# An attention-and-gated-MLP kernel: y returned in transposed form, gating and spatial sums read PSUM on VectorE, late u, a plain first spatial product

## The chip, the cores and the metric

The kernel runs on one core of one Trainium2 chip. The metric is device time in microseconds. In the profile PE is TensorE (PEld its weight loads), DVE is VectorE, ACT is ScalarE, POOL is GpSimd, SP is SyncE, which issues the DMAs.

## The reference

B = 4 batches, H = 8 heads, S = 768 tokens, D = 48. A linear attention with decay, and behind it a gated MLP that mixes tokens:

```python
for t in range(S):                                   # r, k, v: (B, H, S, D)
    cur = einsum('bhd,bhe->bhde', u * k[t], v[t])
    y[:, :, t] = einsum('bhd,bhde->bhe', r[t], state + cur)
    state = w[:, :, None] * state + einsum('bhd,bhe->bhde', k[t], v[t])
x = y as (B, S, 384)
h = maximum(x @ w_in, 0)                             # 384 -> 1024
u, v = h[..., :512], h[..., 512:]
v_n = (v - mean(v)) / sqrt(var(v) + 1e-6)            # over the 512 features
v_s = einsum('ts,bsd->btd', w_spatial, v_n) + b_spatial
out = (u * v_s) @ w_out                              # 512 -> 384
```

All is fp32. The large products are done as three products of high and low parts (high x high, high x low, low x high); such a triple is called `mm3`. A value that goes into such a product is first split: a cast gives the high part, and a subtraction the low part.

## The kernel before

**Scheduling.** The program does not emit instructions directly. `op()` records an operation with the engines that may do it and a planned duration on each. `plan.run()` then simulates the engines: TensorE takes the ready operation that was written first, the other engines take by due time, and an operation that VectorE or GpSimd may do goes to one of them by these rules. `plan.issue()` emits the result, so each engine has a fixed order. Buffers come from numbered groups (`gF` ten 128x384 buffers for u, sums and outputs; `gAB` ten double ones for split operands; `gX` four for x; `gM` four PSUM banks, shown as `pm`; `ps` and `xp` two banks each). An operation that needs a slot waits for the last reader of what was in it.

**Attention.** A batch has six chunks of 128 tokens, 24 in all, and `attend(m)` does one: `prep` scales k and r by the decays (L513, 128x512 each), makes the products r k u (L515, L516; for the first seven chunks `prod` on L522 and column sums on TensorE, L532) and ks (L517), and from their sums dg (L538) the diagonal blocks of the matrix a (`dia`, L541). `g0` (L548 from `s`) multiplies r of the first 64 tokens with the carried state. `g1` makes the scores (L578) and the state's gains (L586) in `ps`. `mid` merges the scores into a with a predicated copy (L595) and forms t1, ub and s2, the state after 64 and after 128 tokens (L603, L607, L609). `g2` (L548) adds t1's share for the second 64 tokens and a x v, both into `xp`, as y with tokens on the partitions. Then yh (a cast, ACT or DVE) and yl = y - yh follow (L636 on VectorE; in the first seven chunks L631 on TensorE and a copy), and `turn` (L650) transposes both through TensorE with an identity, from where they are copied (L309 on ACT or L313 on DVE) into xh and xl, the halves of x. A half batch (three chunks) has one xh and one xl.

**MLP.** `moe_v` (one per chunk, nine 128x512 matmuls, L660 to L662) gives v; relu, statistics and scales follow (L684 to L717), and the normalization runs on ACT (L724) or DVE (L726). `moe_u` (half batch t, feature block d) gives u by nine 128x384 matmuls, copied to SBUF with relu. The spatial product over 768 tokens runs in seven products instead of eight, `moe_sp(b, k, n)`, with k a pair of feature blocks and n the unit:

```python
UNITS = {1: ("X", "11", "11"), 7: ("Y", "s3", "t3"), 5: ("Z", "s1", "t1"), 2: ("X", "12", "21"),
         6: ("Y", "s2", "t2"), 4: ("Y", "22", "t4"), 3: ("Z", "s4", "22")}
```

The three entries are the PSUM bank, the data operand and the weight operand. A unit is nine 128x384 matmuls (L809). Its data operands are blocks of v or sums of them (`s3`, L739; `tail`, L754), each split by `apart` (high on ACT, low part L734 on DVE or POOL). Its weight operands are blocks of the spatial weights or differences of them (`conv_sp`, L479), split likewise (L475 the low part). The sums behind a unit are on L821: with a PSUM operand they run on VectorE, with both operands in SBUF on VectorE or GpSimd:

```python
op({"V": vec(TH)} if xp else VP, lambda e: e.tensor_tensor(out=o(), in0=x(), in1=y(), op=alu),
```

`gate` then multiplies the sum by u in SBUF (L790), and splits the result, gt (ACT, and L793 for the low part). `moe_out` multiplies gt by w_out (twelve 128x384 matmuls), and the result is copied (`ob`) and stored.

**Order.** Batch 0's chunks 0 to 6 are written by hand among the conversions of the weights and the first v and u units. From there a list `seq` holds the units of all batches (v, outputs of the batch before, u, spatial units), and an attention step is put in after every 34/6 of its units.

Of the kernel before, what the change touches and what calls it, by code (L numbers as in the profile page):

```python
# [75 lines left out]

class Plan:
# [81 lines left out]
    def run(self, t0, late=0.4):  # L159
# [3 lines left out]
        idle = {e: 0.0 for e in "EAVPS"}  # L163
        wire = 0.0
# [5 lines left out]
        while pend:  # L170
            while True:
                began = False
                for e in "EAVPS":
# [3 lines left out]
                    for o in ready:  # L177
# [7 lines left out]
                        k = o.i if e == "E" else o.due  # L185
# [8 lines left out]
                    idle[e] = t + o.eng[e]  # L194
                    o.end = idle[e] + o.lag
# [58 lines left out]
def fused_kernel(ctx, tc, rkT, rkvN, wT, uB, w_in, w_sp, b_sp, w_out, out):  # L254
# [34 lines left out]
    def vec2(n):  # L289
        return (n + 150) / 960 + 0.09  # L290
# [32 lines left out]
    eye, neg, one = fixed([P, P], "eye"), fixed([P, P], "neg", F32R), fixed([P, P], "one", F32R)  # L323
    diag, mask, w128 = fixed([P, HC], "diag"), fixed([P, 2, HC], "mask"), fixed([P, NP], "w128")
# [3 lines left out]
    ws = {n: fixed([P, 2, 3, TH], f"ws{n}", F32R) for n in ("11", "21", "22", "t1", "t2", "t3", "t4")}  # L328

# [7 lines left out]
    def load_chunk(m, parts):  # L337
# [29 lines left out]
    def raw_out(k):  # L367
        raws["out", k] = buf = Buf(gAB, [P, 2 * TH], U32, "raw", "c", 3)
# [32 lines left out]
    op({"A": sb(128)}, lambda e: e.mul(neg(), eye(), -1.0), r=[eye], w=[neg], name="neg")
    op({"A": sb(128)}, lambda e: e.copy(one(), eye()), r=[eye], w=[one], name="one")

    def turn_tt(p, z, s0):
        pt = Buf(gM, [P, 512], F32, "pm", "t", 1)

        def f(e):
            for j in range(2):
                hd, o = slice(64 * j, 64 * j + 64), s0 ^ 64 * j
                e.matmul(pt()[o:o + 64, 0:64], tt()[hd, p, s0:s0 + 64], eye()[hd, hd], start=True, stop=True,  # L410
                         skip_group_check=True)

        op({"E": 0.2}, f, r=[tt, eye], psum=[pt], name="tn")
        acopy((tn, (p, z)), lambda: tn()[:, p, z, :], pt, lambda: pt()[:, 0:D], D, True, "tn", {"V": vec(D)})
# [65 lines left out]

    def conv_sp(i):
# [24 lines left out]
    def prep(m):  # L506
# [10 lines left out]
        op(VP, lambda e: e.tensor_tensor(out=kn()[:, 0:DM], in0=kn()[:, 0:DM], in1=tn().rearrange("s p z d -> s (p z d)"),  # L517
# [507 lines left out]
```

## Time and profile before

| | |
|---|---|
| three runs | 403.17, 397.26, 399.00 us; median 399.0 us |
| profiled execution | 399.85 us, its span 398.0 us |
| TensorE clock granted, mean | 0.965 |
| busy share PE, DVE, ACT, POOL | 91%, 77%, 38%, 60% |
| instructions in the span | 11111 |
| DMA | 38.66 MB, mean 97 GB/s |

The page gives the busy time of each engine over the span, the clock in 40 slices, the groups of instructions that cost most and, for each, the idle time ahead of it with what ended it. A share is a mean over the span: weights are loaded and converted, and batch 0 runs, in about its first third, and the outputs of batch 0 begin at 138 us.

### The profile page before, as it was taken

The page shows a single profiled execution, that of the slowest core. Times are in us where ns is not written, and L with a number is a line of the kernel's source. Part 1 is how long each engine was busy: PE and PEld are TensorE (multiplying, and loading weights), DVE is VectorE, ACT ScalarE, POOL GpSimd, SP SyncE. Part 2 cuts the span into 40 slices and gives each one's busy share as a digit, 9 for nine tenths or more (in the row PEclk, how much of TensorE's full clock was granted, in tenths as well). Part 3 has the DMA queues.
Part 4 walks back from the last instruction along what each step waited for, and adds up shares of the span by engine and source line. Part 5 has one row for each costly group of instructions (what it writes and reads, how often), then busy time and mean ns, then how long its engine had stood idle before and what let it go on. Part 6 is the DMA issues. An engine that isn't in the chain of part 4 may idle for free.

```text
span 398.0 us, 11111 instructions
## 1 busy us (share of the span) xinstructions
PE 361.5 (91%) x4686; PEld 330.6 (83%) x4686; DVE 304.6 (77%) x522; ACT 149.8 (38%) x355; POOL 240.5 (60%) x210
## 2 busy tenths in 40 slices
PE   2989999977977699998997999999979999999996
PEld 1868797876976699987987899888879899989996
DVE  4958899998999962769999744789999913579840
ACT  3436464734343221434341312336241322443421
POOL 4877887994998850756997423338998400116520
PEclk9989998986999999999998999999998999999999
DMA  7998255502120243252222334324031011000012
GB/s 227 336 294 273 74 155 173 182 23 91 26 91 0 83 132 99 76 161 70 94 68 68 95 112 135 102 68 145 20 114 49 2 61 41 21 0 2 1 34 86
DMA packets 24385, 38.66 MB, mean 97 GB/s; under 512 B 2960, under 2 KB 16528, under 8 KB 24336
## 3 DMA queue, kind: packets, MB, share of 16 engines
q1 hardware_dynamic: 24336, 37.96, 30.2%
q8 instruction: 37, 0.61, 0.7%
q14 instruction: 12, 0.10, 0.1%
HBM read 33.23 MB, written 4.72 MB: 95 GB/s over the span
## 4 chain that ended last, share of the span: by engine, by line
PE 52%; DVE 32%; issue 6%; POOL 4%; DMA 3%; ACT 1%; SPq 1%; DVEq 0%; POOLq 0%
PE pm L660 11%; PE pm L661 10%; PE pm L662 10%; PE pm L809 6%; PE xp L548 6%; DVE tp L821 5%; DVE ab L734 4%; DVE sf L754 3%; PE pm L650 2%; PE ps L578 2%; PE ps L586 2%; DVE v L726 1%; DMA uw<-wT 1%; DVE u L790 1%; PE pm L456 1%
## 5 line engine op out<-in xcount | busy, mean ns | idle before, releaser
L809 PE MATMUL pm<-wst,ab 128*128 128x384 f32 x288 | 59.2, 351 | 4.5 <-DVE ab L734 2.0
L809 PEld LDWEIGHTS pm<-wst,ab 128*128 128x128 f32 x288 | 52.0, 196 | 6.8 <-DVE ab L734 3.0
L809 PE MATMUL pm<-ws,ab 128*128 128x384 f32 x216 | 43.8, 352 | 0.0
L734 POOL TENSOR_TENSOR ab<-v,ab 128x384 fp32r<-128x384 f32 x19 | 23.4, 1233 | 32.2 <-ACT ab L309 32.2
L809 PEld LDWEIGHTS pm<-ws,ab 128*128 128x128 f32 x216 | 39.3, 196 | 0.2
L660 PE MATMUL pm<-xh,wiuh 128*128 128x384 f32 x96 | 34.9, 363 | 0.0
L660 PE MATMUL pm<-woh,gt 128*128 128x384 f32 x96 | 33.8, 352 | 0.0
L309 ACT CAST gt<-u 128x384 fp32r<-128x384 f32 x32 | 16.3, 515 | 44.5 <-POOL u L790 22.9
L662 PE MATMUL pm<-xh,wiul 128*128 128x384 f32 x96 | 33.1, 344 | 0.0
L661 PE MATMUL pm<-xl,wiuh 128*128 128x384 f32 x96 | 33.0, 344 | 0.0
L661 PE MATMUL pm<-wol,gt 128*128 128x384 f32 x96 | 32.9, 343 | 0.0
L662 PE MATMUL pm<-woh,gt 128*128 128x384 f32 x96 | 32.8, 342 | 0.0
L660 PE MATMUL pm<-wivh,xh 128*128 128x512 f32 x72 | 30.3, 421 | 1.0 <-DVE tp L821 0.7
L513 POOL TENSOR_TENSOR rT<-rT,tt 128x512 f32<-128x512 f32 x21 | 29.8, 1418 | 1.5 <-DMA rT<-rkT 1.3
L516 POOL TENSOR_TENSOR rn<-rn,ub 128x384 f32<-128x384 f32 x11 | 12.0, 1093 | 29.3 <-DVE rn L515 26.6
L661 PE MATMUL pm<-wivl,xh 128*128 128x512 f32 x72 | 28.7, 399 | 0.0
L662 PE MATMUL pm<-wivh,xl 128*128 128x512 f32 x72 | 28.7, 399 | 0.0
L309 ACT COPY ob<-pm 128x384 f32<-128x384 f32 x24 | 11.5, 480 | 40.9 <-PE pm L662 40.9
L548 PEld LDWEIGHTS xp<-t,rT 64*64 64x64 f32 x384 | 13.8, 137 | 15.3 <-issue 13.7
L793 POOL TENSOR_TENSOR gt<-u,gt 128x384 fp32r<-128x384 f32 x17 | 20.6, 1214 | 9.9 <-ACT gt L309 9.9
L695 DVE BATCH_NORM_STATS2 q<-v 128x6 f32<-128x512 f32 x18 | 12.4, 688 | 17.5 <-ACT v L309 17.5
L548 PE MATMUL xp<-t,rT 64*64 64x48 f32 x384 | 16.7, 225 | 9.2 <-DVE t L603 9.2
(156 smaller groups left out, 992.0 us busy)
## 6 DMA issues: line engine op xcount, KB each, us to landing
kT<-rkT SPq DMA_DIRECT2D x24, 256.0 KB, 3.4
rT<-rkT SPq DMA_DIRECT2D x24, 256.0 KB, 3.2
kn<-rkvN SPq DMA_DIRECT2D x24, 200.0 KB, 2.7
vn<-rkvN SPq DMA_DIRECT2D x24, 192.0 KB, 3.6
out<-ob SPq DMA_DIRECT2D x24, 192.0 KB, 1.9
rn<-rkvN SPq DMA_DIRECT2D x17, 192.0 KB, 2.4
wst<-w_sp SPq DMA_DIRECT2D x12, 192.0 KB, 3.2
raw<-w_in SPq DMA_DIRECT2D x4, 384.0 KB, 5.5
```

The costliest lines, as they stand in the source:

```text
L309: e.activation(out=o_f(), in_=i_f(), func=func) if func else e.copy(o_f(), i_f())
L513: op(eng, lambda e, x=x: e.tensor_tensor(out=x(), in0=x(), in1=tt(), op=ALU.mult), r=[tt], w=[x], name="scale")
L516: op(VP, lambda e: e.tensor_tensor(out=rn()[:, 0:DM], in0=rn()[:, 0:DM], in1=ub(), op=ALU.mult), r=[ub], w=[rn], name="rku")
L548: e.matmul(xp[t0:t0 + 64, j, p * D:(p + 1) * D], lhsT, rhs, start=(z, j) not in began, stop=True, skip_group_check=True, tile_position=(ro ...
L660: e.matmul(o, lh, rh, start=first, stop=False)
L661: e.matmul(o, lh, rl, start=False, stop=False)
L662: e.matmul(o, ll, rh, start=False, stop=last)
L695: op({"V": 0.69}, lambda e: e.bn_stats(out=q6()[:, i, :], in_=vf()[:, i]), r=[(vf, i)], w=[(q, ("s", i))], name="stats")
L734: op(VP, lambda e: e.tensor_tensor(out=t()[:, 1], in0=src(), in1=t()[:, 0].bitcast(F32), op=ALU.subtract), r=[(t, 0), src_b], w=[(t, 1)], ...
L793: op(VP, lambda e: e.tensor_tensor(out=gt()[:, 1], in0=u(), in1=gt()[:, 0].bitcast(F32), op=ALU.subtract), r=[(gt, 0), u], w=[(gt, 1)], na ...
L809: e.matmul(pm(), a()[:, x, i], w()[:, y, i], start=not began and i + q_ == 0, stop=i + q_ == 4, skip_group_check=True)
L821: op({"V": vec(TH)} if xp else VP, lambda e: e.tensor_tensor(out=o(), in0=x(), in1=y(), op=alu), r=[yb] if xp else [xb, yb], w=[o], psum=[ ...
```

## The change

**y comes back transposed.** `g0`, its small fence copy and `turn` are gone. `g2` now puts v and the state on the other side of the matmul, so that features stand on the partitions of `xp`, in tiles of 32 columns; xh and xl come directly from `xp`. For this the carried state is held as block-diagonal pairs of heads in `sb_98` and `sb_99`, filled by four ACT copies a chunk (two from s, two from t1).

```diff
+    def block(z, src_b, src, ps):
+        for o, q_ in ((0, 0), (64, D)):
+            acopy((sblk[z], o), lambda o=o, q_=q_: sblk[z]()[o:o + 64, :, q_:q_ + D], src_b, lambda o=o: src()[o:o + 64], 192, ps, "block")
...
     def g2(m):
+        quads = [(jt, g, *((jt, g) if g < 3 else (3, jt))) for jt in range(NK) for g in range(4)]
...
+            def mm(z, g, jt, row, lhsT, rhs):
+                e.matmul(x[32 * g:32 * g + 32, z, jt * HC:(jt + 1) * HC], lhsT, rhs, start=(z, g) not in began, stop=True,
+                         skip_group_check=True, tile_position=(row, 32 * g))
+            for z, s0, t0 in SUBS:
+                if z or c:
+                    for jt, g, p, k in quads:
+                        mm(z, g, jt, 0, sblk[z]()[:, p, 32 * k:32 * k + 32], r[:, p, t0:t0 + 64])
+            for jt, g, p, k in quads:
+                for j, e0 in ((0, 32 * k), (1, 32 * (k - 1))):
+                    if (k < 2 if j == 0 else k > 0):
+                        for z, s0, t0 in SUBS:
+                            mm(z, g, jt, s0, v[s0:s0 + 64, 2 * p + j, e0:e0 + 32], a[s0:s0 + 64, j, p, :])
```

v's rows are padded to 64 columns a head for it (192 KB a chunk become 256). From chunk 8 on, the diagonal blocks are made by eight small ACT products a chunk instead of one operation on VectorE or GpSimd.

**Gates and sums read PSUM.** In `late` the u matmuls come after the spatial sum; one VectorE operation then does relu and gate on the PSUM bank, a cast on ACT gives gt's high part and VectorE subtracts it from the same bank. In `moe_sp` every sum of a unit has a PSUM operand now, and the units' order is 1, 5, 6, 7, 2, 4, 3:

```diff
+    def late(b, t, d):
+        pm = Buf(gM, [P, 512], F32, "pm")
+        x = xsum[b, t, d]
...
+        op({"V": vec(TH)}, lambda e: e.scalar_tensor_tensor(out=uv(), in0=uv(), scalar=0.0, in1=x(), op0=ALU.max, op1=ALU.mult), ...
+        acopy((gt, 0), lambda: gt()[:, 0], pm, uv, TH, True, "gt hi")
+        op({"V": vec(TH)}, lambda e: e.tensor_tensor(out=gt()[:, 1], in0=uv(), in1=gt()[:, 0].bitcast(F32), op=ALU.subtract), ...
...
         if n == 1:
-            acopy(x1, lambda: x1(), pb, pm, TH, True, "tp")
-            plus(x2, sbt(x1), B2)
-            plus(x1, sbt(x1), B1)
+            plus(x1, acc, B1)
+            plus(x2, acc, B2)
...
         elif n == 6:
-            plus(x2, acc, sbt(x2))
-            plus(g22, (zb, lambda: zb()[:, 0:TH], True), sbt(x2))
-            plus(p7, sbt(x2), sbt(p7), ALU.subtract)
-            gate(b, 1, k + 2, g22)
+            plus(x3, acc, sbt(x2))
+        elif n == 7:
+            plus(x2, acc, sbt(x2))
+            plus(x2, (zb, lambda: zb()[:, 0:TH], True), sbt(x2))
+            gate(b, 1, k + 2, x2)
```

**Batch 0's product is plain.** It uses the weights' four blocks (`conv_std`, 12 splits) and eight units of 18 matmuls (`moe_std`), with the bias added from PSUM. The differences of the weights (`conv_t`) follow in batch 1, behind its third and fourth v unit. Batch 0's u is early for its first half of the tokens, and late for its second half.

**Order and planning.** From chunk 7 on, attention steps have written places in the list, outputs stand between v units singly or in threes, and w_out's conversion starts at the list's units 1 to 4. The normalization is on ACT alone, `gF` has seven buffers, `gX` five. In `run()` an operation that GpSimd could do gets a due time 2 us later for VectorE (`GAIN`), and two operations of VectorE and GpSimd on SBUF at the same time are charged more (`held`).

```diff
-            seq += v[0:1] + last[0:3] + v[1:2] + last[3:6] + v[2:3] + dr + u[0][0:2] + v[3:4] + u[0][2:3] + v[4:6] + \
...
+            seq += v[0:1] + A[4:5] + v[1:2] + last[0:1] + v[2:3] + dr + A[5:6] + last[1:2] + v[3:4] + last[2:3] + v[4:6] + \
+                [lambda b=b: tail(b, 0)] + last[3:6]
+            seq += [p[0][1], p[0][5], p[0][6], p[0][7], lambda b=b: direct(b, 1), A[6], p[0][2], lt[1][2], p[0][4],
+                    lambda b=b: tail(b, 1), A[7], lt[0][0], p[0][3], lt[0][2]]
```

Three places show what moves. The first is TensorE where batch 0's last v unit ends and its spatial product begins. Before, the last two attention steps ahead of the last v unit were these (`t_1237`, `t_1333` are t1 of two chunks, `neg` the negative identity, `one` the identity):

```order
L548 MATMUL xp<-t_1237,rT 64x48 x8
L548 MATMUL xp<-vn,a 64x48 x16
L578 MATMUL ps<-rT,kT 64x64 x16
L586 MATMUL ps<-vn,kn 64x48 x16
L631 MATMUL xp<-yh,neg 128x192 x2
L650 MATMUL pm<-one,yh 128x128 x3
L650 MATMUL pm<-one,yl 128x128 x3
L548 MATMUL xp<-t_1333,rT 64x48 x8
L548 MATMUL xp<-vn,a 64x48 x16
```

Now, between the last v unit and the first unit of the plain product (`ws_91` is the weight block 11), TensorE's order has:

```order
L639 MATMUL xp<-rT,sb_99 32x64 x12
L639 MATMUL xp<-a,vn 32x64 x32
L585 MATMUL ps<-rT,kT 64x64 x16
L593 MATMUL ps<-vn,kn 64x48 x16
L664 MATMUL xp<-xh,neg 128x192 x2
L585 MATMUL ps<-rT,kT 64x64 x16
L593 MATMUL ps<-vn,kn 64x48 x16
L639 MATMUL xp<-rT,sb_98 32x64 x12
L639 MATMUL xp<-rT,sb_99 32x64 x12
L639 MATMUL xp<-a,vn 32x64 x32
L675 MATMUL pm<-ws_91,ab 128x384
```

The turn is gone, a g2 has 44 to 56 matmuls instead of 24, and two g1 and two g2 stand ahead of the first plain unit, where four u units stood before.

The second place is TensorE in the first pair of feature blocks of batch 1's spatial product. Before (`ws_93` is unit 2, `wst_95` unit 5, `wst_96` unit 6):

```order
L548 MATMUL xp<-s_2561,rT 64x48 x8
L578 MATMUL ps<-rT,kT 64x64 x16
L586 MATMUL ps<-vn,kn 64x48 x16
L650 MATMUL pm<-one,yh 128x128 x3
L809 MATMUL pm<-ws_93,ab 128x384 x9
L650 MATMUL pm<-one,yl 128x128 x3
L809 MATMUL pm<-wst_95,ab 128x384 x9
L809 MATMUL pm<-wst_96,ab 128x384 x9
L548 MATMUL xp<-t_2782,rT 64x48 x8
```

Now (`ws_91` unit 1, `wst_94` unit 5, `wst_95` unit 6, `wst_96` unit 7, `ws_92` unit 2):

```order
L867 MATMUL pm<-ws_91,ab 128x384 x9
L867 MATMUL pm<-wst_94,ab 128x384 x9
L867 MATMUL pm<-wst_95,ab 128x384 x9
L585 MATMUL ps<-rT,kT 64x64 x16
L593 MATMUL ps<-vn,kn 64x48 x16
L867 MATMUL pm<-wst_96,ab 128x384 x9
L867 MATMUL pm<-ws_92,ab 128x384 x9
L639 MATMUL xp<-rT,sb_99 32x64 x12
L639 MATMUL xp<-a,vn 32x64 x32
```

Units 6 and 7 share the bank Y, and a g1 stands between them.

The third place is VectorE in the same stretch, behind batch 1's first units. Before:

```order
L790 TENSOR_TENSOR u<-u,tp 128x384
L821 TENSOR_TENSOR tp<-tp,bb 128x384
L821 TENSOR_TENSOR tp<-pm,tp 128x384 x2
L636 TENSOR_TENSOR yl<-xp,yh 128x384
L821 TENSOR_TENSOR tp<-tp 128x384
L754 TENSOR_TENSOR sf<-v 128x384
```

Now, a little further on in it (`pm<-pm,tp` is relu and gate in PSUM, `gt<-pm,gt` the low part):

```order
L834 SCALAR_TENSOR_TENSOR pm<-pm,tp 128x384
L560 TENSOR_REDUCE dg<-rn 128x4x2
L879 TENSOR_TENSOR tp<-pm,tp 128x384
L838 TENSOR_TENSOR gt<-pm,gt 128x384
L611 COPY_PREDICATED a<-mask,ps 128x512
L618 TENSOR_TENSOR t_2963<-s_2807,ps 128x192
```

The gate, the sum and the low part each have a PSUM operand; the sums with both operands in SBUF are gone. At the end of the batch VectorE's order is:

```order
L834 SCALAR_TENSOR_TENSOR pm<-pm,tp 128x384 x2
L838 TENSOR_TENSOR gt<-pm,gt 128x384 x2
L669 TENSOR_TENSOR xl<-xp,xh 128x2x3x64
L318 TENSOR_SCALAR v<-pm 128x512
L535 TENSOR_TENSOR rT<-rT,tt 128x512
L710 BN_STATS q<-v 128x6
L611 COPY_PREDICATED a<-mask,ps 128x512
```

One xl subtraction stands directly ahead of this piece, and four more follow within the next 40 rows.

More of the change, by code (lines that the diff above doesn't have):

```diff
@@ L194, in run @@
                     idle[e] = t + o.eng[e]
+                    if e in "VP" and o.port:
+                        other = "P" if e == "V" else "V"
+                        if held[other] > t:
+                            idle[e] += (0.65 if e == "V" else 0.4) * min(o.eng[e], held[other] - t)
+                        held[e] = idle[e]
                     o.end = idle[e] + o.lag
@@ L322, in fused_kernel @@
     ub = fixed([P, DM], "ub")
-    eye, neg, one = fixed([P, P], "eye"), fixed([P, P], "neg", F32R), fixed([P, P], "one", F32R)
-    diag, mask, w128 = fixed([P, HC], "diag"), fixed([P, 2, HC], "mask"), fixed([P, NP], "w128")
+    eye, neg = fixed([P, P], "eye"), fixed([P, P], "neg", F32R)
+    diag, mask, w128 = fixed([P, HC], "diag"), fixed([P, HC], "mask"), fixed([P, NP], "w128")
     bb = fixed([P, S], "bb")
@@ L479, in combine, with conv_std, conv_t @@
         op(VP, lambda e: e.tensor_tensor(out=o(), in0=x(), in1=y(), op=ALU.subtract), r=[x, y], w=[o], name="wsum")
+    def conv_std(t, i):
+        for s_ in range(2):
+            raw_sp(s_, t, i)
+            part(("11", "12", "21", "22")[2 * s_ + t], i, raws["sp", s_, t, i])
+    def conv_t(i):
+        for k in ((0, 0), (0, 1), (1, 1), (1, 0)):
+            raw_sp(*k, i)
+        x11, x12, x22, x21 = (raws["sp", *k, i] for k in ((0, 0), (0, 1), (1, 1), (1, 0)))
+        combine(x11, x12, x11)
+        combine(x12, x22, x12)
+        part("t3", i, x12)
+        part("t1", i, x11)
+        combine(x11, x22, x11)
+        part("t2", i, x11)
+        combine(x21, x21, x11)
+        part("t4", i, x21)
     def conv_sp(i):
@@ L546, in y_mm @@
-    def y_mm(e, t, z, t0, p, j, row, lhsT, rhs):
-        xp, began = t["xp"](), t["began"]
-        e.matmul(xp[t0:t0 + 64, j, p * D:(p + 1) * D], lhsT, rhs, start=(z, j) not in began, stop=True, skip_group_check=True,
-                 tile_position=(row, t0))
-        began.add((z, j))
-    def carry(e, t, z, s):
-        t0 = 64 * z
-        for p in range(NP):
-            for j in range(2):
-                hd = slice(64 * j, 64 * j + 64)
-                y_mm(e, t, z, t0, p, j, 64 * j, t["r"]()[hd, p, t0:t0 + 64], s()[hd, p, :])
@@ L628, in g2 @@
         if m < YPE:
             def low(e):
-                for j in range(2):
-                    e.matmul(y()[:, j], neg(), yh()[:, j], start=False, stop=True, skip_group_check=True)
-            op({"E": 0.2}, low, r=[neg, yh], psum=[xp], name="yneg")
-            acopy(yl, lambda: yl(), xp, y, DM, True, "yl")
-        else:
-            op({"V": vec(DM)}, lambda e: e.tensor_tensor(out=yl(), in0=y(), in1=yh().bitcast(F32), op=ALU.subtract), r=[yh],
-               w=[yl], psum=[xp], name="yl")
@@ L896, in attend @@
         prep(m)
-        g0(m)
         g1(m)
@@ L900, in attend @@
         g2(m)
-        turn(m)
     attend(0)
@@ L917, in fused_kernel @@
     moe_v(0, 2)
-    s3(0), direct(0, 0), direct(0, 1)
+    for d in range(4):
+        plain(0, 0, d)
     for d in range(2):
@@ L1001 @@
     ut[:, :D] = u.reshape(NP, 2, D).transpose(1, 2, 0)
-    uz = np.zeros((2, 64, NP, 2, D), u.dtype)
-    for z in range(2):
-        for j in range(2):
-            uz[1 - z ^ j, :, :, z] = u.reshape(NP, 2, D)[:, j]
-    pairs = np.arange(DM).reshape(NP, 2, D).transpose(1, 0, 2).reshape(DM)
+    rows = [np.concatenate([np.arange(2 * j * D, (2 * j + 2) * D), np.arange(6 * D + 32 * j, 6 * D + 32 * j + 32)])
+            for j in range(NK)]
     arrays = {
```

305 lines of the change are left out of this document (162 added, 143 removed).

## The prediction

> **What bounds the kernel now.** I read the page's busy shares first, then the windows before and after the end of the first batch's spatial product, then TensorE's (PE's) waits, then its timeline at one stall.
>
> ```profile
> PE 361.5 (91%) x4686; PEld 330.6 (83%) x4686; DVE 304.6 (77%) x522; ACT 149.8 (38%) x355; POOL 240.5 (60%) x210
> ```
> ```profile
> core 0: us, PE busy (x) PEld busy (x) DVE busy (x) ACT busy (x) POOL busy (x), PEclk, DMA share, GB/s
> 0.00:10.00 10.00, 2.10 (x37) 1.59 (x38) 4.28 (x11) 3.40 (x13) 4.91 (x16) 1.00 0.72 228
> 10.00:138.00 128.00, 111.64 (x1817) 98.64 (x1815) 116.46 (x191) 58.25 (x148) 107.09 (x91) 0.93 0.44 139
> 138.00:398.00 260.00, 247.72 (x2844) 230.33 (x2839) 183.82 (x322) 88.19 (x194) 128.48 (x105) 0.98 0.23 72
> ```
> The 91% hides two kernels. From 138 us on, PE is busy 247.7 of 260 us at clock 0.98: it is the bound. From 10 to 138 us VectorE (DVE) is busy 116.5 of 128 us and GpSimd (POOL) 107.1, together 223.6 of 256; PE sits idle 16.4 us there and runs at 0.93, so about another 0.07 x 128 = 9 us go to a slow clock. Some 25 us of the first stretch are therefore not matmul work.
>
> The waits of PE, first list 10 to 138 us, second list after it (total us, times, longest):
>
> ```profile
> PE xp L548 <- DVE t L603: 6.2, 3, 3.1
> PE pm L650 <- DVE xh L313: 2.5, 1, 2.5
> ```
> ```profile
> PE xp L548 <- DVE t L603: 3.0, 1, 3.0
> PE pm L650 <- DVE yl L636: 2.3, 2, 2.0
> ```
> What ends last is nearly always a VectorE result, and it is late because VectorE's queue is full, as at the start of batch 0's spatial product on PE's timeline:
>
> ```profile
> 93.78 0.95 PE L548 MATMUL xp<-t,rT 64*64 64x48 f32 x13 [2.90 <-DVE t L603]
> ...
> 95.65 3.25 PE L809 MATMUL pm<-ws,ab 128*128 128x384 f32 x9
> 98.69 1.70 PE L809 MATMUL pm<-wst,ab 128*128 128x384 f32 x5
> ```
> The stall costs 2.90 us, and the nine matmuls behind it take 98.69 - 95.65 = 3.04 us at the lowered clock.
>
> **Matmul work, removed and added.** One clean stretch of PE's timeline prices the attention step (g0 is L548 from s, g1 is L578 and L586, g2 is L548 from t and vn, the turn is L650):
>
> ```profile
> 227.75 0.44 PE L650 MATMUL pm<-one,yh 128*128 128x128 f32 x3
> 228.03 0.50 PE L650 MATMUL pm<-one,yl 128*128 128x128 f32 x3
> 228.37 0.39 PE L660 MATMUL pm<-woh,gt 128*128 128x384 f32 x1
> ...
> 234.84 0.49 PE L548 MATMUL xp<-s,rT 64*64 64x48 f32 x10
> 235.12 0.27 PE L578 MATMUL ps<-rT,kT 64*64 64x64 f32 x1
> ...
> 235.35 0.59 PE L578 MATMUL ps<-rT,kT 64*64 64x64 f32 x26
> 235.73 0.25 PE L586 MATMUL ps<-vn,kn 64*64 64x48 f32 x1
> ...
> 238.11 0.39 PE L661 MATMUL pm<-wivl,xh 128*128 128x512 f32 x1
> 238.34 0.40 PE L662 MATMUL pm<-wivh,xl 128*128 128x512 f32 x1
> 238.66 0.60 PE L548 MATMUL xp<-t,rT 64*64 64x48 f32 x13
> ...
> 239.73 0.44 PE L660 MATMUL pm<-woh,gt 128*128 128x384 f32 x1
> ```
> The turn of one chunk takes 228.37 - 227.75 = 0.62 us and goes for all 24: **-14.9 us**. g2 now takes 239.73 - 238.66 = 1.07 us for 48 records (24 f32 matmuls, two records each). A record in a stream over all four 64x64 quadrants takes (235.73 - 235.35)/26 = 14.6 ns; over two quadrants, as in g0, (235.12 - 234.84)/10 = 28 ns, so g0's 16 records are worth 0.45 us. Old g0 and g2 together: 20 x 0.45 + 24 x 1.07 = 34.7 us.
>
> The new g2 has 24 carry matmuls of 128 rows by 32 columns (12 in a batch's first chunk) and 32 of 64 by 32: 112 records, or 88. No such tile shape is in this trace. The bounds are 28 ns a record (pairs that overlap only two deep) and, since eight tiles can be in flight in the second part, half of 14.6 there. I take 14.6, the nearest stream, keep the fixed 1.07 - 48 x 0.0146 = 0.37 us of the old g2, and add one more change of tile shape, priced at the step into g2: (238.66 - 238.34) - (238.34 - 238.11) = 0.09 us. That is 2.1 us, or 1.75 in a first chunk: 20 x 2.1 + 4 x 1.75 - 34.7 = **+14.3 us** (+3 at the low bound, +49 at 28 ns). The Trainium skill, TensorEngine Tiling (Array Packing), "Tiling Modes", says that a change of mode, not of tile, drains the engine; the 0.09 us above is what this trace shows of such a change, and without it the sum would be 2.2 us lower.
>
> Batch 0's product loses its seven-product form: 8 units of 18 matmuls for 14 of 9, that is 18 more. The stretch
>
> ```profile
> 109.60 3.34 PE L809 MATMUL pm<-ws,ab 128*128 128x384 f32 x18
> 112.77 1.75 PE L809 MATMUL pm<-wst,ab 128*128 128x384 f32 x9
> ```
> gives 3.17/18 = 176 ns each: **+3.2 us**. Matmul work as a whole moves by +2.6 us, which is nothing; the time must come from the stalls.
>
> **Vector work, 10 to 138 us.**
>
> ```profile
> L821 DVE TENSOR_TENSOR tp<-pm,tp x32: 543/548/559, 106.5 to 382.2; 128x384 f32<-128x384 f32 x32
> L821 DVE TENSOR_TENSOR tp<-tp,bb x7: 540/1343/1375, 187.2 to 373.6; 128x384 f32<-128x384 f32 x7
> L790 POOL TENSOR_TENSOR u<-u,tp x15: 997/1327/1464, 109.0 to 382.9; 128x384 f32<-128x384 f32 x15
> ```
> ```profile
> L475 POOL TENSOR_TENSOR wst<-wst,wst 128x384 fp32r<-128x384 f32 x8 | 9.7, 1224 | 1.8 <-ACT wst L309 1.8
> L479 POOL TENSOR_TENSOR wst<-wst 128x384 f32<-128x384 f32 x8 | 9.0, 1125 | 1.2 <-DVE ws L475 0.6 <-issue 0.5
> L734 POOL TENSOR_TENSOR ab<-v,ab 128x384 fp32r<-128x384 f32 x6 | 7.4, 1239 | 2.2 <-ACT ab L309 2.2
> L313 DVE CAST xh<-pm 128x384 fp32r<-128x384 f32 x4 | 2.2, 546 | 1.4 <-PE pm L650 1.4
> ```
> These give two prices (ns min/median/max above, mean below). A VectorE sum with one operand in PSUM never leaves 543 to 559 ns; the same sum with both in SBUF has a median of 1343, and on GpSimd 1327: about 1.2 us either way. By the code, batch 0 needs 75 such SBUF operations now (33 for the weights' low parts and differences, 6 and 14 in the tails, 6 sums, 16 for gates) and 28 afterwards (12, 8, 8); 24 more weight operations move to batch 1's start, and the queues' order puts about half of those still in this stretch. So 75 - 28 - 12 = 35 fewer, 42 us; PSUM sums on VectorE go from 10 to 16, +3.3 us, and about as much goes with the six casts of xh and xl. 223.6 becomes some 182 us. At today's share (223.6/256 = 87%) the two engines would need 104 us for what takes 128; PE's own floor there is 128 - 25 = 103. Both floors say up to 25 us; I take **-18**, because the new order leaves only two g1 (64 records, 0.93 us each) and two g2 (1.75 and 2.1), 5.7 us, to cover batch 0's normalization, where four u units stand today.
>
> **After 138 us.** Idle and slow clock there are 260 - 247.7 + 0.02 x 260 = 17 us, of which the last 3 are the final store. Per batch, 22 SBUF operations (26 us on either engine) become PSUM ones (from 10 to 32, 12 us more on VectorE). What is added: ScalarE takes all three norms, eight small products for each chunk from 8 on, and four block copies a chunk:
>
> ```profile
> L724 ACT ACTIVATE v<-v,q 128x512 f32<-128x512 f32 x11 | 8.7, 812 | 12.1 <-DVE q L717 9.0 <-DVE q L715 3.1
> L388 ACT COPY tt<-tmp 128x252 f32<-128x252 f32 x1 | 0.4, 403 | 0.7 <-DVE tmp L385 0.7
> L401 ACT ACTIVATE neg<-eye 128x128 fp32r<-128x128 f32 x1 | 0.3, 294 | 0.0
> ```
> From 294 ns for 128 and 403 for 252 columns, 64 columns cost 0.24 and 192 cost 0.35 us: 128 x 0.24 + 88 x 0.35 = 61 us, less what ScalarE loses in copies; it stays under half busy. Two of the block copies (0.7 us) stand between t1 and g2, covered by the unit that PE has queued there; uncovered they are 24 x 0.7 = 17 us. VectorE's wait for unit 6's bank before unit 7 is hidden too: PE's order has a g1 or unit 2 between them. A u unit that comes late keeps its PSUM buffer through a gate, a cast and a low part, 1.6 us longer, and who queues behind it is the next v or output; u also keeps xh and xl. I take **-4** (between -14 and +5). The first 10 us and the loads (vn a third larger, the spatial weights twice) I price at 0: the DMA share is 0.44 and below where they move to.
>
> **Sum** against the profiled execution, 399.85 us (span 398.0; 0.2% above the median 399.0, so no correction): 399.85 + 2.6 - 18 - 4 = **380 us**.
>
> **Rivals.**
> - *The 32-column tiles do not overlap like the 64x64 ones* (slower). For it: g0's 28 ns with two quadrants. Against: 14.6 ns where four tiles alternate, as four do in the new order. Each ns a record is worth 20 x 0.112 + 4 x 0.088 = 2.6 us. From 25 ns on the time passes 407, slower by 2%; at 28 ns it is 380 + 13.4 x 2.6 = 415. Chance 0.11. The Trainium skill, TensorE: Matmul & The Clock Gate, "Wait — 56ns, not 53.3ns?", gives a floor of about 25 ns from start to start however small the matmul; by it the time would be 407. The 14.6 ns of this trace stand against it for 64x64 tiles, and no row here has a 32-column one.
> - *The waits move to the batch boundaries* (no difference). With u late, x's five buffers (two per half batch) hold back the next batch's attention, and its chunks bunch at the boundary; batch 0's start has little cover. One episode like the one at 93.78 us costs 2.90 + 3.04 - 9 x 0.176 = 4.4 us; four make 380 + 17 = 397. For it: five xl subtractions stand close together in VectorE's new order. Against: outputs and v units lie between them. Chance 0.19.
> - *Nearly all stalls go*: 25 in the first stretch, 9 in the second, g2 at its low bound: 399.85 - 9 - 25 - 9 = 357. Chance 0.10.
>
> **How the numbers follow.** The forecast (370 to 391) has the other 0.60. The range 360 to 399 leaves out half of the last rival, all of the first and a bit of the second. 2% (8 us) is about what a measurement can tell from no change: faster 0.60 + 0.10 = 0.70, within 0.19, slower 0.11.
>
> **What would show it.** g2 of one chunk near 2.1 us on PE and no turn; VectorE and GpSimd busy together under 190 us up to the first output; the first output's matmuls near 120 us instead of 138; PE's clock above 0.95 in that stretch; PSUM gates at 0.55 us; PE idle after that under 12 us. I am wrong if g2 takes over 2.8 us, or if PE's idle time gathers where batches meet.

## The result, and the profile after

The changed kernel takes **373.6 us** (median of 4 runs, 370.7 to 377.5) where the kernel before takes 401.1 (4 runs on the same chip): ratio **0.930, interval 0.918 to 0.942**. The forecast was 380 (0.95 of 399.85) with a range of 360 to 399. Timed once more in the experiments below it has 0.9385 (0.933 to 0.944), which is the base that they are compared with. (Medians are of all executions, while the ratios leave disturbed ones out, so the two can differ by a per cent.) The profiled execution has 373.19 us with a span of 371.5; before it had 399.85 and 398.0.

The page's busy shares, and the windows of the changed kernel (columns as before):

```profile
PE 343.1 (92%) x5652; PEld 310.8 (84%) x5652; DVE 271.5 (73%) x513; ACT 178.0 (48%) x478; POOL 173.4 (47%) x158
```
```profile
10.00:138.00 128.00, 112.88 (x2340) 97.75 (x2344) 107.25 (x193) 72.18 (x195) 86.56 (x77) 0.95 0.55 175
138.00:371.50 233.50, 228.78 (x3318) 212.08 (x3310) 159.59 (x311) 102.86 (x276) 81.47 (x66) 1.00 0.25 77
```
Over the span PE's busy time falls by 18.4 us, and its idle time from 36.5 to 28.4 us. The two stretches share this unequally. From 10 to 138 us PE idles 15.1 us (16.4 before). From 138 us to the end it idles 4.7 us of 233.5, where it was 12.3 of 260, and its clock is 1.00 there instead of 0.98. PE's waits, first list 10 to 138 us, second list from there to the end:

```profile
PE ps L585 <- DVE s L625: 7.4, 1, 7.4
PE xp L639 <- ACT sb L316: 3.8, 4, 1.6
PE ps L585 <- issue: 1.5, 1, 1.5
```
```profile
PE xp L639 <- issue: 1.1, 1, 1.1
```
All that is left behind 138 us is one wait of 1.1 us and the final store. In the first stretch one stall of 7.4 us stands alone. On PE's timeline it is ahead of batch 0's spatial product:

```profile
79.59 0.63 PE L593 MATMUL ps<-vn,kn 64*64 64x48 f32 x32
80.35 0.47 PE L664 MATMUL xp<-xh,neg 128*128 128x192 f32 x2
88.25 1.13 PE L585 MATMUL ps<-rT,kT 64*64 64x64 f32 x32 [7.43 <-DVE s L625]
89.13 1.08 PE L593 MATMUL ps<-vn,kn 64*64 64x48 f32 x32
90.14 1.51 PE L639 MATMUL xp<-rT,sb 128*32 128x64 f32 x48
91.58 1.67 PE L639 MATMUL xp<-a,vn 64*32 64x64 f32 x64
93.17 0.66 PE L675 MATMUL pm<-ws,ab 128*128 128x384 f32 x1
```
Behind the stall the granted clock is 0.50 from 88.25 to 93.17 us: one g1 (L585 and L593) and one g2 (L639) take 4.92 us there. The attention step on PE in clean stretches, first g1, then g2, and then the g2 of a batch's first chunk:

```profile
119.23 0.69 PE L585 MATMUL ps<-rT,kT 64*64 64x64 f32 x32
119.75 0.63 PE L593 MATMUL ps<-vn,kn 64*64 64x48 f32 x32
120.31 0.44 PE L675 MATMUL pm<-ws,ab 128*128 128x384 f32 x1
```
```profile
220.87 0.88 PE L639 MATMUL xp<-rT,sb 128*32 128x64 f32 x48
221.68 0.97 PE L639 MATMUL xp<-a,vn 64*32 64x64 f32 x64
222.58 0.44 PE L675 MATMUL pm<-woh,gt 128*128 128x384 f32 x1
```
```profile
171.06 0.54 PE L639 MATMUL xp<-rT,sb 128*32 128x64 f32 x24
171.53 0.97 PE L639 MATMUL xp<-a,vn 64*32 64x64 f32 x64
172.43 0.44 PE L675 MATMUL pm<-xh,wiuh 128*128 128x384 f32 x1
```
g1 takes 120.31 - 119.23 = 1.08 us, g2 takes 222.58 - 220.87 = 1.71 us and 1.37 in a first chunk. So the stall's episode costs 7.43 + 4.92 - 1.08 - 1.71 = 9.6 us. In g2 there are 48 records of the carry at 16.9 ns and 64 of a x v at 14.1 ns. The groups on VectorE that read PSUM (sum, gate, low part):

```profile
L879 DVE TENSOR_TENSOR tp<-pm,tp 128x384 f32<-128x384 f32 x30 | 16.6, 553 | 4.4 <-PE pm L867 4.2
L834 DVE SCALAR_TENSOR_TENSOR pm<-pm,tp 128x384 f32<-128x384 f32 x28 | 15.6, 559 | 9.3 <-PE pm L677 9.2
L838 DVE TENSOR_TENSOR gt<-pm,gt 128x384 fp32r<-128x384 f32 x28 | 15.5, 552 | 6.2 <-ACT gt L316 5.8
```
Each costs 0.55 to 0.56 us, as priced.

### The profile page after: what moved, and what is told of

Same layout as the page of the kernel before. It is cut to its first block, busy times and chain, and to the rows that moved or that the text cites. A ratio compares the mean times of both kernels' runs of the same rounds, so it can differ in the third digit from the quotient of the medians.

```text
span 371.5 us, 13095 instructions
## 1 busy us (share of the span) xinstructions
PE 343.1 (92%) x5652; PEld 310.8 (84%) x5652; DVE 271.5 (73%) x513; ACT 178.0 (48%) x478; POOL 173.4 (47%) x158
## 4 chain that ended last, share of the span: by engine, by line
PE 87%; DVE 4%; POOL 3%; ACT 2%; issue 2%; DMA 1%; SPq 1%; POOLq 0%; DVEq 0%; ACTq 0%
PE pm L867 18%; PE pm L675 17%; PE pm L677 15%; PE pm L676 15%; PE xp L639 10%; PE ps L585 4%; PE ps L593 3%; PE pm L460 2%; DMA raw<-w_in 1%; PE pm L554 1%; POOL wst L483 1%; POOL rn L537 1%; SPq L303 1%; POOL a L569 1%; ACT v L739 1%
## 5 line engine op out<-in xcount | busy, mean ns | idle before, releaser
L316 ACT CAST gt<-pm 128x384 fp32r<-128x384 f32 x28 | 13.4, 479 | 82.7 <-DVE pm L834 79.1
L867 PE MATMUL pm<-wst,ab 128*128 128x384 f32 x216 | 41.9, 341 | 0.0
L867 PEld LDWEIGHTS pm<-wst,ab 128*128 128x128 f32 x216 | 37.7, 188 | 0.8 <-issue 0.2
L566 ACT ACTIVATE a<-diag,dg 128x64 f32<-128x64 f32 x128 | 32.8, 337 | 2.5 <-DVE dg L560 2.3
L539 POOL TENSOR_TENSOR kn<-kn,tn 128x384 f32<-128x384 f32 x14 | 17.2, 1227 | 30.5 <-DVE rn L537 24.3
L676 PE MATMUL pm<-wivl,xh 128*128 128x512 f32 x72 | 28.4, 394 | 0.0
L535 POOL TENSOR_TENSOR kT<-kT,tt 128x512 f32<-128x512 f32 x17 | 23.9, 1407 | 6.8 <-DMA kT<-rkT 4.7
L585 PE MATMUL ps<-rT,kT 64*64 64x64 f32 x768 | 18.7, 232 | 9.0 <-DVE s L625 7.4
L585 PEld LDWEIGHTS ps<-rT,kT 64*64 64x64 f32 x768 | 15.2, 141 | 13.8 <-issue 12.9
L639 PEld LDWEIGHTS xp<-rT,sb 128*32 128x32 f32 x1056 | 17.1, 112 | 11.5 <-ACT sb L316 5.8
L639 PE MATMUL xp<-rT,sb 128*32 128x64 f32 x1056 | 22.1, 226 | 4.2 <-ACT sb L316 3.8
```

Source lines behind the costliest of these rows:

```text
L316: e.activation(out=o_f(), in_=i_f(), func=func) if func else e.copy(o_f(), i_f())
L535: op(eng, lambda e, x=x: e.tensor_tensor(out=x(), in0=x(), in1=tt(), op=ALU.mult), r=[tt], w=[x], name="scale")
L566: op({"A": sb(64)}, lambda e, j=j, p=p: e.mul(a()[:, j, p, :], diag(), dg()[:, j, p:p + 1]), r=[diag, (dg, j)], w=[(a, (j, p))], name="dia")
L585: e.matmul(ps[s0:s0 + 64, j, p * HC:(p + 1) * HC], k[hd, p, s0:s0 + 64], r[hd, p, t0:t0 + 64], start=True, stop=True, skip_group_check=True)
L639: e.matmul(x[32 * g:32 * g + 32, z, jt * HC:(jt + 1) * HC], lhsT, rhs, start=(z, g) not in began, stop=True, skip_group_check=True, tile_p ...
L676: e.matmul(o, lh, rl, start=False, stop=False)
```

## The experiments

The question after the result: is it the matmul work, the work taken off VectorE and GpSimd (which the prediction held for the main cause), or the order? The first run is the base, and the next three change one thing each.

**The changed kernel again** (`again`), no edit, as the base.

> The changed kernel itself, once more, as the base of the other runs. 371 to 376 us, ratio 0.925 to 0.94, span near 371.5 us; TensorE idle near 28 us of the span, of which one stall of about 7.4 us where batch 0's spatial product begins.

Measured: 376.7 us, ratio 0.9385 (0.9333 to 0.9437). The median is just above what was expected and the ratio within it; the stall is there again (7.5 us).

**The tiles' order in g2** (`group`).

```diff
-quads = [(jt, g, *((jt, g) if g < 3 else (3, jt))) for jt in range(NK) for g in range(4)]
+quads = [(jt, g, *((jt, g) if g < 3 else (3, jt))) for g in range(4) for jt in range(NK)]
```

> The same 44 to 56 matmuls of g2, in an order in which those of one 32-column group follow each other instead of alternating over the four groups. Theory A (0.0169 and 0.0142 us a record come from the overlap of tiles in different column groups): a record costs 0.028 us as in the old g0 or more, g2 goes from 1.71 to about 3.1 us, 20 x 1.4 + 4 x 1.1 = 32 us more, 405 us (395 to 430). Rival B (small matmuls start at a fixed distance, whichever tile they use): g2 stays at 1.7 us, 371 to 376 us.

Measured: 390.5 us, ratio 0.974 (0.968 to 0.980). On PE's timeline:

```profile
218.21 1.51 PE L639 MATMUL xp<-rT,sb 128*32 128x64 f32 x48
219.66 1.42 PE L639 MATMUL xp<-a,vn 64*32 64x64 f32 x64
221.00 0.44 PE L675 MATMUL pm<-woh,gt 128*128 128x384 f32 x1
```
The same matmuls now take 2.79 us: the carry 30 ns a record, a x v 21. So the price of a small tile hangs on its neighbours, and theory A holds in kind. The time stays below its range: a x v, whose matmuls still alternate over two row halves, grew by only half of what A had, and PE waits less. PE's busy time grows by 24 us (367.4 against 343.1). Of these, 18.5 show between the two profiled spans (390.0 and 371.5) and 14 between the medians (390.5 and the base's 376.7). PE's idle time falls from 28.4 to 390.0 - 367.4 = 22.6 us, by this row of the whole span,

```profile
0.00:390.00 390.00, 367.42 (x5652) 336.60 (x5652) 266.55 (x513) 178.47 (x478) 171.97 (x158) 0.99 0.35 110
```
which fits that what PE waited for comes ready while the longer g2 runs.

**Gates in SBUF** (`gate_sbuf`), in `late`:

```diff
-        op({"V": vec(TH)}, lambda e: e.scalar_tensor_tensor(out=uv(), in0=uv(), scalar=0.0, in1=x(), ...
-        ...
+        u = us[b, t, d] = Buf(gF, [P, TH], F32, "u")
+        acopy(u, lambda: u(), pm, uv, TH, True, "u", {"V": vec(TH)}, AF.Relu)
+        gate(b, t, d, x)
```

> Late u and the order of TensorE stay; but u is copied to SBUF with relu and the gate and its low part run there again, on VectorE or GpSimd (28 gates: 56 operations of 0.55 us on VectorE become 56 of about 0.8 to 1.3 us on either engine, and ScalarE gets 28 copies). Theory A (the change gains by taking such work off the two engines, which had made TensorE wait): some 36 us more work on the two, TensorE's idle time grows, 381 us (377 to 387). Rival B (TensorE's own order and work make the gain, and VectorE and GpSimd have room now, 73% and 47% busy): 371 to 376 us.

Measured: 375.9 us, ratio 0.938 (0.932 to 0.945): no difference from the base. The operations did become dearer, by these rows of VectorE and GpSimd,

```profile
L845 DVE TENSOR_TENSOR u<-u,tp 128x384 f32<-128x384 f32 x23 | 20.2, 879 | 12.3 <-ACT u L316 12.2
L848 POOL TENSOR_TENSOR gt<-u,gt 128x384 fp32r<-128x384 f32 x20 | 21.7, 1087 | 37.9 <-ACT gt L316 37.9
```
0.88 and 1.09 us where PSUM cost 0.55, and GpSimd's busy time behind 138 us goes from 81.5 to 106.9 us, but PE's listed waits there come to only 2.4 us. Theory A falls for the gates.

**Differences of the weights held back** (`hold`).

```diff
-        op(VP, lambda e: e.tensor_tensor(out=o(), in0=x(), in1=y(), op=ALU.subtract), ..., name="wsum")
+        op(VP, lambda e: e.tensor_tensor(out=o(), in0=x(), in1=y(), op=ALU.subtract), ..., name="wsum", after=first[0:1])
...
-        op({"E": 3.15}, f, r=a + w, psum=[pm], name="std")
+        first.append(op({"E": 3.15}, f, r=a + w, psum=[pm], name="std"))
```

> Only the differences of the spatial weights (needed in batch 1) are held back until batch 0's first plain unit. Theory A (the stall of 7.4 us ahead of that product is VectorE's and GpSimd's queue: a dozen such operations run between 66 and 86 us, ahead of and beside batch 0's scales, in which an operation on 3 numbers takes up to 1.19 us): the stall falls to 2 to 3 us, 367 us (364 to 370). Rival B (it is the latency of the normalization's own chain, with too little matmul work beside it): the stall stays over 6 us and the time at 372 or more. Rival C (the held work comes due later and stalls batch 1): the stall goes, another of the same size comes at 115 to 165 us, 372 to 376.

Measured: 376.8 us, ratio 0.931 (0.924 to 0.938), which overlaps the base's interval. The stall's rows, and one further on, are now

```profile
78.82 0.47 PE L666 MATMUL xp<-xh,neg 128*128 128x192 f32 x2 [1.28 <-ACT xh L316]
84.13 1.13 PE L587 MATMUL ps<-rT,kT 64*64 64x64 f32 x32 [4.85 <-DVE s L627]
...
122.60 1.23 PE L641 MATMUL xp<-rT,sb 128*32 128x64 f32 x24 [2.89 <-ACT sb L316]
```
The stall itself is 2.6 us shorter, but a wait of 1.28 us now stands ahead of it, so about 1.3 us were the weights' differences in the queue. PE's idle time over the span hardly moves (27.6 against 28.4 us). A has a small part of the stall and B most of it, as `cover_hold` below bears out. C has its later wait, 2.89 us at 122.6 us and so smaller than C had it, where the changed kernel lists none between 93 and 180 us; the first output begins at 136.0 us, no earlier than with the change (135.6).

The next four asked where the gain is.

**Transposed y alone** (`y_only`): the attention of the changed kernel in the program of the kernel before. Against the changed kernel:

```diff
-GAIN = 2.0
-DIA = lambda m: m > 7
+GAIN = 0.0
+DIA = lambda m: False
...
-    gF, gAB, gV = group("f", 7), group("ab", 10), group("v", 2)
-    gX = group("x", 5)
+    gF, gAB, gV = group("f", 10), group("ab", 10), group("v", 2)
+    gX = group("x", 4)
...
-            seq += v[0:1] + A[4:5] + v[1:2] + last[0:1] + v[2:3] + dr + A[5:6] + last[1:2] + ...
+            seq += v[0:1] + last[0:3] + v[1:2] + last[3:6] + v[2:3] + dr + u[0][0:2] + ...
```

> One part alone: y in transposed form (new g2, block copies, no g0 and no turn, the padded v rows), with the MLP, the order of the program, the planner's rules and the group sizes of the kernel before (xh and xl as four buffers, ten in gF). Theory A (part of the gain is here: 24 x 0.43 = 10 us of matmul work, and the 9 us that TensorE idled ahead of the turn and of g0, behind VectorE's xh, yl and copies): 399.9 - 10 - 9 = 381 us (377 to 385). Rival B (only the matmul work goes, since VectorE's queue makes TensorE wait elsewhere): 390 us (387 to 394). Rival C (the whole gain is here, the rest of the change moves nothing): 371 to 376 us.

Measured: 395.6 us, ratio **0.989** (0.986 to 0.992). Less gain than any theory gave. PE's waits from 10 to 138 us, then from 138 us to the end, show why:

```profile
PE xp L664 <- ACT xh L316: 7.9, 4, 2.4
PE pm L828 <- DVE tp L840: 2.6, 2, 2.4
PE pm L675 <- DVE u L318: 2.2, 1, 2.2
```
```profile
PE xp L639 <- ACT sb L316: 4.2, 3, 2.4
PE pm L828 <- POOL ab L749: 2.7, 3, 1.0
PE pm L828 <- DVE tp L840: 2.1, 1, 2.1
```
The waits ahead of the turn are gone, as forecast for them, and results of ScalarE, VectorE and GpSimd now end waits ahead of the spatial units (L828), ahead of the new carry (L639, behind the block copies) and ahead of the low part of x (L664, behind xh). PE's busy time falls by 361.5 - 353.9 = 7.6 us, but its idle time is 394.0 - 353.9 = 40.1 us, 3.6 more than the 36.5 before: about half of what went came back as waiting. Rival B, and a little more.

**Batch 0 with seven products again** (`seven0`).

```diff
-    for i in range(3):
-        conv_std(0, i)
+    conv_sp(0)
     moe_v(0, 5)
+    conv_sp(1)
+    tail(0, 0)
+    conv_sp(2)
     attend(6)
...
+            seq += pq[0][0:4] + at[0:1] + pq[0][4:5] + lt[2:3] + pq[0][5:6] + [lambda: tail(0, 1)] + at[1:2] + pq[0][6:7] + lt[0:1]
+            seq += pq[1][0:4] + at[2:3] + pq[1][4:5] + lt[3:4] + pq[1][5:7] + lt[1:2]
```

Here pq are the units of a pair, at the attention steps 7 to 9, lt the late u.

> The changed kernel, but batch 0's spatial product is again of seven products, with late u for its second half, and all 36 weight operations in batch 0 instead of 12 there and 24 held for batch 1. Matmul work falls by 18 x 0.176 = 3.2 us. Theory A (VectorE and GpSimd are the bound up to the first output, so the 24 weight operations and the sums of v there cost more than the matmuls save): 380 us (377 to 388). Rival B (TensorE's work decides there too, as after it): 370 to 374 us.

Measured: 377.3 us, ratio 0.943 (0.938 to 0.948). The 3.2 us of matmul work that it saves are lost in the first stretch:

```profile
10.00:138.00 128.00, 110.90 (x2298) 94.88 (x2299) 113.21 (x194) 72.08 (x196) 101.34 (x89) 0.92 0.49 154
```
VectorE and GpSimd are busy 214.5 us there instead of 193.8, PE idles 17.1 instead of 15.1, at clock 0.92 instead of 0.95. By the centres the plain product is worth 0.5%, and the intervals overlap. The median lies at the lower edge of theory A's range, but not apart from the base.

**Gates and sums in SBUF** (`all_sbuf`): `gate_sbuf`, and the sums of the kernel before behind units 1, 7, 6 and 3, for which unit 7 goes back to its place ahead of 5 and 6:

```diff
-            plus(x1, acc, B1)
-            plus(x2, acc, B2)
+            acopy(x1, lambda: x1(), pb, pm, TH, True, "tp")
+            plus(x2, sbt(x1), B2)
+            plus(x1, sbt(x1), B1)
```

> The changed kernel with both the gates (as in the run before with u copied to SBUF) and the sums behind the units (the old form with p7: two more copies on ScalarE and three sums in SBUF a pair, of which there are six) on SBUF operands again: some 36 + 18 x 1.2 - 18 x 0.55 = 48 us more on VectorE and GpSimd together. Theory A (the two have room after the first output, 72% and 47% busy, and TensorE's order is what counts): 373 to 379 us. Rival B (this is where the room ends): over 382 us.

Measured: 374.5 us, ratio 0.937 (0.931 to 0.944): theory A. The windows from 138 us on:

```profile
138.00:372.70 234.70, 229.29 (x3320) 212.53 (x3318) 166.65 (x290) 117.52 (x306) 117.50 (x100) 1.00 0.25 77
```
VectorE and GpSimd do 284 us of work there instead of 241, and PE idles 5.4 us instead of 4.7. Reading PSUM in gates and sums, alone, moves nothing that these runs can tell.

**The planner's two rules off** (`plan0`).

```diff
-GAIN = 2.0
+GAIN = 0.0
...
-                        if held[other] > t:
+                        if False:
```

> The changed kernel with the planner's two new rules off (the 2 us by which VectorE leaves an operation to GpSimd, and the charge for running both on SBUF at once). Theory A (the rules move a few operations between two engines that have room): 372 to 378 us. Rival B (they keep GpSimd's work out of the way of VectorE's PSUM operations, on which TensorE waits): 380 us or more.

Measured: 377.1 us, ratio 0.943 (0.937 to 0.949): theory A. By the centres it is 0.5%, and the intervals overlap.

The last four split what lies between transposed y alone and the whole.

**The order alone** (`order_alone`): the changed kernel with the edits of `all_sbuf`, `seven0`, `plan0` and `dia_norm` (below) together, which is `y_only` with the new list and the new group sizes.

> Transposed y, and of the rest only the order: attention steps at written places, outputs singly between v units, u late (copied to SBUF, gates and sums on SBUF operands as before), gX of five and gF of seven buffers. Undone are the PSUM operands, the plain product, the diagonal blocks and the normalization on ScalarE, and the planner's two rules, so VectorE and GpSimd have about the work that they had with transposed y alone (308 and 220 us). Theory A (the 20 us between transposed y alone, 395.6 us, and the whole change come from the order): 377 us (372 to 383). Rival B (they come from the work taken off VectorE and GpSimd as a whole, though neither the gates and sums nor the plain product showed it alone): 388 us or more.

Measured: 385.7 us, ratio **0.959** (0.954 to 0.964), between the two theories. The order, with late u and the group sizes in it, is worth 0.989 - 0.959 = 3.0% of 401 us, 12 us; all offloads together, down to 0.9385, are worth another 2.1%, 8 us. Which of PE's waits the order removed is not shown: the one trace of this run is of its longest execution, 393.38 us.

**u early again** (`early_u`): `moe_u` at its old places, `gX` 4 and `gF` 10 as before; attention steps and outputs stay where the change puts them.

```diff
-    gX = group("x", 5)
+    gX = group("x", 4)
...
-            seq += v[0:1] + A[4:5] + ... + v[2:3] + dr + A[5:6] + last[1:2] + v[3:4] + last[2:3] + v[4:6] + ...
+            seq += v[0:1] + A[4:5] + ... + v[2:3] + dr + u[0][0:2] + A[5:6] + last[1:2] + v[3:4] + u[0][2:3] + last[2:3] + v[4:6] + ...
```

> The changed kernel, but u of batches 1 to 3 stands where it stood before, ahead of the spatial units, copied to SBUF and gated there; with four buffers in gX and ten in gF as before. Attention steps and outputs keep their written places. Theory A (of the 10 us that the order was worth on top of transposed y, 395.6 to 385.7, most is u behind its sum: no wait of u's buffers, and the two halves of x are read late, between the units): 382 us (379 to 388). Rival B (the written places of the attention steps and of the outputs make it): 372 to 378 us.

Measured: 379.4 us, ratio 0.946 (0.939 to 0.954). The median is just inside theory A's range and above B's, but the base itself has 376.7. Early u costs some 0.8% by the centres, 3 us, with its gates in SBUF and the old group sizes in it, and the intervals overlap. That is less than theory A had (most of 10 us), and does not decide for B. If the parts add up, most of the order's 3% is not u's place; what is left of the list is the written places of the attention steps and outputs, which no run moved alone.

**Diagonal blocks and normalization off ScalarE** (`dia_norm`).

```diff
-DIA = lambda m: m > 7
+DIA = lambda m: False
...
-            op({"A": sb(DH)}, norm, r=[(q, "rs")], w=[(vf, k)], name="norm")
+            op({"A": 0.81, "V": 0.45}, norm, r=[(q, "rs")], w=[(vf, k)], name="norm")
```

> The changed kernel with the diagonal blocks as one operation on VectorE or GpSimd (1.1 to 1.2 us for each of 16 chunks, in place of 128 products of 0.34 us on ScalarE) and the normalization on ScalarE or VectorE by the planner's choice (24 operations of 0.76 to 0.81 us): some 27 us more on VectorE and GpSimd. Theory A (it is this work, the largest that ScalarE took over, that makes the 10 us between the order alone, 385.7 us, and the whole change): 381 us (378 to 386). Rival B (like the gates and sums it fits into the room that the two engines have; the 10 us need all of the offloads together): 372 to 377 us.

Measured: 375.9 us, ratio 0.936 (0.929 to 0.944): no difference from the base, as B has it. None of the four offloads (gates and sums, plain product, ScalarE's share, planner) shows alone; together they are 8 us. This can be room that is used up only when all are back. It can also be four gains of some 2 us that add up: each ratio is known to some 0.6% either way, 2.4 us, and so is the base's. No run with two or three of them back was made, so this stays open.

**Cover for batch 0's normalization** (`cover_hold`): `hold`, and

```diff
     moe_v(0, 5)
+    moe_u(0, 1, 0)
+    moe_u(0, 1, 1)
     attend(6)
```

These two leave the list's late u units, so the matmul work stays the same.

> The changed kernel with the differences of the weights held back (as in the run before that did so) and two u units of batch 0's second half, 3.2 us of matmuls, ahead of attention step 6, where batch 0's normalization runs. Theory A (what is left of the stall, 4.85 us with the differences held, is the chain from the last v unit through statistics, scales and normalization, with nothing of TensorE's beside it): the stall falls by about 3 us to under 2, and the time to 369 us (366 to 372) where the changed kernel has 372 to 376. Rival B (VectorE's queue ends the stall and gets two more casts or gates ahead of it): the stall stays at 4 us or more, no change.

Measured: **370.3 us, ratio 0.923** (0.918 to 0.928), below the base's interval. Against `hold` alone (0.924 to 0.938) the intervals just overlap, and the wide interval of the changed kernel's first timing (0.918 to 0.942) takes this one in. On PE's timeline the stall is 2.71 us, not quite theory A's 2, and the first plain unit follows at once:

```profile
79.57 0.63 PE L595 MATMUL ps<-vn,kn 64*64 64x48 f32 x32
82.91 0.47 PE L666 MATMUL xp<-xh,neg 128*128 128x192 f32 x2 [2.71 <-ACT xh L316]
83.21 0.36 PE L677 MATMUL pm<-ws,ab 128*128 128x384 f32 x1
```
What is left of the stall is still the normalization, now on ScalarE: the cast xh, for which PE waits, stands behind the three normalizations and a cast in ScalarE's queue.

```profile
79.71 2.22 ACT L741 ACTIVATE v<-v,q 128x512 f32<-128x512 f32 x3 [0.96 <-DVE q L732]
81.97 0.51 ACT L316 CAST ab<-v 128x384 fp32r<-128x384 f32 x1
82.38 0.47 ACT L316 CAST xh<-xp 128x384 fp32r<-128x384 f32 x1
```
The slow clock behind the stall goes too: the granted clock is 1.00 from 83.21 to 93 us, where `hold` has 0.51 behind its stall, from 84.13 to 88.91 us. The first output begins at 128.6 us instead of 135.6, and from 10 to 138 us PE is now busy 119.2 of 128 us at clock 0.97. By these runs this version is faster than the kernel before and than the base.

## Why the prediction was right

**The matmul sum was too high by 9 us.** The failed step is the price of the new g2: 2.1 us and +14.3 in all. Measured, 20 x 1.71 + 4 x 1.37 - 34.7 = +5.0. The records' 14.6 ns was right (14.1 and 16.9). Wrong was the "fixed 0.37 us" kept from the old g2, and 0.09 for the change of tile on top. The old g2's 16 carry records ran over two quadrants, at the 28 ns that the prediction itself read from g0; with 16 x 0.028 + 32 x 0.0146 = 0.92 of its 1.07 us nearly nothing was fixed. The new carry uses four column groups, and its records cost 16.9 ns. Matmul work moves by -14.9 + 5.0 + 3.2 = -6.7 us, not +2.6. That term alone would have put the forecast at 371.

**The slow-tile rival** (415 us) fell: in the new order a record takes 14.1 and 16.9 ns on average. `group` shows that it could have: in another order of the same tiles the carry costs 30 ns. By the Trainium skill, TensorE: Matmul & The Clock Gate, "Wait — 56ns, not 53.3ns?", no start follows another within about 25 ns; the 14.1 and 16.9 ns here are under that, and where consecutive tiles share their columns, 30 is above it and 21 under it, so for small tiles side by side the measurement speaks against the rule.

**The stalls were sized rightly as a sum and put in the wrong place, so the sum is right by luck.** Forecast -18 and -4, together -22; measured, 373.19 - 399.85 + 6.7 = -20. But in the first stretch, where -18 was put, PE's idle time fell by 1.3 us and its clock rose by 0.02 of 128 us, some 4 us together. Behind 138 us, where -4 was put, idle time fell by 7.6 us, and 0.02 of 260 us of clock are 5 more. (These leave 3 us of the 20 without a place; the clock is read to two digits.) VectorE and GpSimd did go from 223.6 to 193.8 us (forecast 182) in the first stretch. A part of what is missing is the price of 1.2 us for an operation with all operands in SBUF on either engine: VectorE's gates before took 0.80 us on average,

```profile
L790 DVE TENSOR_TENSOR u<-u,tp 128x384 f32<-128x384 f32 x17 | 13.7, 803 | 0.4
```
But the step that failed is the one from there to PE's floor. PE did not wait for the two engines' sum of work but for single results: the 7.4 us are one chain. On VectorE's timeline inside that stall, ahead of the state's update (L625) for which PE waits, stand the scales of batch 0's normalization:

```profile
83.98 0.49 DVE L725 TENSOR_TENSOR q<-q 128x3 f32<-128x3 f32 x1
84.50 0.92 DVE L726 TENSOR_TENSOR q<-q 128x3 f32<-128x3 f32 x1
85.46 1.19 DVE L727 TENSOR_SCALAR q<-q 128x3 f32<-128x3 f32 x1
...
87.75 0.36 DVE L625 TENSOR_TENSOR s<-ps,w 128x192 f32<-128x192 f32 x1
```
The "little cover" that the prediction allowed 7 us for (25 less 18) is what `cover_hold` fills. Of the 5.7 us of cover that it counted, the second g1 and g2 could not cover: they stand behind the stall (88.25 us), since they need the state that VectorE updates behind the scales. And "the first output near 120 us" was wrong: it begins at 135.6, one v unit and one g1 (3.3 us) later in the order, where it was 138.2 before. Of the other signs, VectorE and GpSimd together were to be under 190 us (193.8), the clock above 0.95 (0.95), the PSUM gates at 0.55 us (0.56) and PE's idle time behind the first output under 12 us (4.7).

**Its reason for the time after 138 us is not borne out.** Written there was that SBUF operations become PSUM ones. They do (0.55 us each), and alone it gives nothing that the runs can tell: `gate_sbuf` and `all_sbuf`. It may have a part in the 2.1% of all offloads together. The order gave more, 3.0% on top of the 1.1% of transposed y. ScalarE's small products took 0.34 us each and not the estimated 0.24, but taking them off it again (`dia_norm`) made no difference that the runs could tell. I had treated the moved attention steps and late u as a risk (the second rival) and priced nothing for what they bring. That rival had its condition right for the first boundary only, one episode of 9.6 us instead of four of 4.4; the later boundaries show no wait above 1.1 us.

**Nothing is as additive as my sum.** Transposed y alone saves 7.6 us of PE's busy time and 4.4 us of time; in `group` 24 us more work cost 14 by the medians and 18.5 by the profiled spans.

## What to carry to other kernels

Price small matmul tiles by the records around them: here records in alternating column groups cost 0.56 (16.9 against 30 ns) and 0.67 (14.1 against 21) of those in the same one, so the loop's order over tiles counts as well as their number. Where an engine is busy nine tenths and its waits end at many different results, taking work off the engines behind it can show little. Here each offload alone was less than a run can tell, all together were worth 2.1%, and the order 3.0%; offloads without the new order were not run. So test the order and the load apart before crediting either. Ask of every boundary what the waited-for engine has queued ahead of the one small result, and what independent matmuls can stand there. A stall also costs the slow matmuls behind it, here 2.1 us behind one of 7.4.

## What the runs showed of the hardware

The tile rates were the surprise (14.1 and 16.9 ns a record alternating over four column groups, 21 and 30 ns with neighbours in one group). The second: VectorE operations on three numbers per partition, 0.16 to 0.18 us elsewhere in the same chain, took 0.49, 0.92 and 1.19 us at 84 to 87 us, while GpSimd ran operations of 0.98 to 1.26 us with all operands in SBUF; a chain of tiny operations is not short beside such work:

```profile
83.19 1.26 POOL L535 TENSOR_TENSOR rT<-rT,tt 128x512 f32<-128x512 f32 x1
84.42 0.98 POOL L537 TENSOR_TENSOR rn<-rn,kn 128x384 f32<-128x384 f32 x1
85.36 1.25 POOL L535 TENSOR_TENSOR kT<-kT,tt 128x512 f32<-128x512 f32 x1
```
GpSimd's three end at 84.45, 85.40 and 86.61 us, and VectorE's three at 84.47, 85.42 and 86.65. In `cover_hold` GpSimd runs nothing from 77.50 to 82.55 us, and the same operations take 0.16 and 0.17 us there. Both fit tiny operations that wait until GpSimd's operation ends; no run varied this alone.
